# Gated linear attention and a two-level mixture of experts: the first expert in parts of 128 and 88 rows, the second in a fixed place, narrow products on halves of the array's columns

## The chip, the cores and the metric

The kernel runs on one core of a Trainium2 chip. The metric is the device time of one execution in microseconds. Three executions of the kernel before took 394.83, 397.62 and 399.1 us; the median is 397.62. The profile is of one further execution, which took 390.5 us.

The engines are TensorE (PE; its weight loads are listed apart as PEld), VectorE (DVE), ScalarE (ACT), GpSimd (POOL) and SyncE (SP). In this kernel SP issues the plain transfers, all in one order, and POOL issues the indirect ones (scatters), among its own arithmetic.

## What is computed

```python
def _attn_ref(q, k, v, alpha):                  # (4, 8, 768, 48) each
    for t in range(S):
        state = alpha[:, :, t, :, None] * state + np.einsum('bhd,bhe->bhde', k[:, :, t], v[:, :, t])
        y[:, :, t] = np.einsum('bhd,bhde->bhe', q[:, :, t], state)

def _moe_ref(x, w_group, w_expert, w1, w2):     # x (3072, 384), G = Eg = 4, F = 1024
    g_idx = np.argmax(x @ w_group, axis=1)
    # g_w: weight of the chosen group by softmax
    for g in range(G):
        # e_idx: argmax of xg @ w_expert[g], e_w its softmax weight
        for e in range(Eg):
            h = np.maximum(xg[mask_e] @ w1[g, e], 0.0)
            ye = h @ w2[g, e]
            out[tok_idx] = (g_w * e_w)[:, None] * ye
```

The result of the attention, (B, H, S, D) turned to 3072 rows of 384, is the x of the mixture. Each row goes to one of 16 experts. Everything is in float32.

## The kernel before, in words

**First stage, the attention, in 24 steps.** The sequence is cut into chunks of 128 rows, 6 for each of 4 batches; step n treats chunk n. On TensorE a step has these pieces, by the names that the plan gives them: OUT (`outputs`, L506: masked scores times v, in the same banks as FB), G (`gains`, L463: the chunk's addition to the state), SC of the next step (`scores`, L428), TR (`turned_keys`, L446: transposed keys), CNT where a group of chunks is to be counted (L601, L605), ROWS (`to_rows`, L527: the chunk's output turned to rows, and the logits of the gates, in one product), FB of the next step (`from_before`, L494: queries times the state). TR is left out where the next chunk but one begins a batch, G and FB where the next one does. L506, L463 and L494 write some partitions from 0 and some from 64, so they already use parts of the array's columns. One matmul of float32 in the program shows as two in the profile.

Around it: q, k and alpha come in units u = 0 to 10 of one to three chunks (transfers L*u*). DVE makes two scans of alpha for each part of a unit (R, F: L378, L388). ACT scales the queries (QS, L405), and the products KP and QP (`decayed`, L414) are made on POOL, or on DVE where the list `BY_DVE` says so. Each step's scores are masked in two halves M0 and M1: the list `MASKS` says how many of them DVE does straight from PSUM (L433); the others are copied by ACT (MC, L856) and masked on POOL (L437).

**The way to the experts.** For groups of chunks DVE picks each row's expert (PA, PB), weighs it (WT) and, after CNT, gives it a place among the expert's slots (PL). X*t* (`scatter`, L625) on POOL then writes the 128 rows of chunk t to `slots_d` in DRAM. The slots are first filled with blank rows (`fill`, four transfers FILL, L320), and every X waits for all of them.

**The plan.** All pieces of the first stage are `Work` items with an engine, a planned duration, needs and a due time. `in_turns` plays them through with these durations and so fixes the order on every engine before the program is built; TensorE's and SP's orders are given by the text. On the chip each engine then runs its list strictly in that order. Constants such as `FIRST`, `STEP`, `X0`, `XSTEP` and `LOGITS` only shift due times or order; `QUEUE` is the order of SP's transfers.

**Second stage, the experts.** `jobs` is a list of (expert, rows). For each, SP reads its rows (`fetch_rows`), DVE transposes them (`columns`, L1031), TensorE makes `hidden_part` (L237: 8 pieces of F by 3 of the model's width) and `result_part` (L248: 3 by 8), ACT takes both out of PSUM, DVE turns the result back and weighs it, and POOL scatters it (L1023). The matmuls move as many columns as the job has rows. Job 0 and job 1 are expert 0: 96 rows that were in place after 12 chunks (`EARLY`, `EARLY_T`), and 128 more. Job 0's hidden products (E0 to E3) and two thirds of its result (RP) belong to the plan and come at the end of the first stage; its rows are read by ER and transposed by ET. The other 15 experts are ordered by their number of rows (`by_number`) and get ceilings of 216, 213, 210 and so on to 168 (`cap`). A loop at the end treats rows above a ceiling. Weights are in two buffers, filled two jobs ahead (`load_weights`); the first is loaded as LW within the plan, job 2's after `by_number`.

```python
    CAP = 224
    FIXED, EARLY, EARLY_T, BLK = 1, 96, (B // 2) * NC, 112
    jobs = [dict(e=0, n=EARLY, rows=early_rows), dict(e=0, c0=EARLY, n=CAP - EARLY)]
    jobs += [dict(r=r, c0=0, n=cap(r)) for r in range(NS)]
```

On these inputs the experts have 213, 184, 202, 191, 211, 196, 184, 200, 180, 158, 195, 181, 168, 194, 205 and 210 rows. Of expert 0's, 96 lie in the first 12 chunks and 131 in the first 16.

Of the kernel before, what the change touches and what calls it, by code (L numbers as in the profile page):

```python
# [96 lines left out]
def gla_then_hierarchical_moe(  # L97
# [53 lines left out]
    FIXED, EARLY, EARLY_T, BLK = 1, 96, (B // 2) * NC, 112  # L151
# [58 lines left out]
    blank = cp.tile([P, 2 * XW], F32, name="blank")  # L210
# [22 lines left out]
    def hidden_part(z, w1, xt, hT, f0, n, halves=(0, 1)):  # L233
        for k in halves:
            f = f0 + k
            for dc in range(DC):
                nc.tensor.matmul(z[:, k * n:(k + 1) * n], lhsT=w1[:, dc, f * P:(f + 1) * P],  # L237
                                 rhs=xt[:, dc, 0:n], start=(dc == 0), stop=(dc == DC - 1))
# [4 lines left out]
    def result_part(z, w2, hT, yT, d0, n):  # L243
        k = min(2, DC - d0)
        for i in range(k):
            dc = d0 + i
            for f in range(FC):
                nc.tensor.matmul(z[:, i * n:(i + 1) * n], lhsT=w2[:, f, dc * P:(dc + 1) * P],  # L248
                                 rhs=hT[:, f, 0:n], start=(f == 0), stop=(f == FC - 1))
# [19 lines left out]
    with ExitStack() as gla:  # L269
# [22 lines left out]
        nc.scalar.copy(out=blank, in_=zeros[:, 0:1].to_broadcast([P, 2 * XW]))  # L292
# [225 lines left out]
        def to_rows(n, yt):  # L518
# [6 lines left out]
            for p in range(HP):  # L525
                at = p * W - p % 2 * NL
                nc.tensor.matmul(z[:, at:at + W], lhsT=yt[:, p, :], rhs=wr[:, p, :],  # L527
                                 start=(p == 0), stop=(p % 2 == 1), skip_group_check=True)
# [8 lines left out]
        def choose(b, c0, c1):  # L537
# [71 lines left out]
            def place():  # L609
# [3 lines left out]
                if cs.stop == EARLY_T:  # L613
                    nc.vector.tensor_scalar(out=new[:, 0:FIXED], in0=new[:, 0:FIXED],
# [38 lines left out]
        def fill(e, n):  # L653
# [3 lines left out]
                in_=blank[0:CAP // 2, None, :].to_broadcast([CAP // 2, n, 2 * XW]))  # L657
# [3 lines left out]
        def constants():  # L661
# [5 lines left out]
            nc.gpsimd.memset(blank.rearrange("p (k w) -> p k w", w=QW)[:, :, QW - 1:QW],  # L667
                             float(4 * N))
# [35 lines left out]
        FIRST, STEP = 11.19, 4.52  # L704
# [4 lines left out]
        BY_DVE = [('QP', 1, 3), ('KP', 3, 3), ('QP', 4, 2), ('QP', 0, 0), ('QP', 3, 3), ('KP', 0, 0), ('QP', 2, 1), ('QP', 1, 2), ('KP', 0, 2), ('QP', 2, 2), ('QP', 3, 2)]  # L709
# [78 lines left out]
        QUEUE = [('L', 1), ('V', 0, 0, 1), ('L', 2), ('L', 3), ('W',), ('V', 0, 1, 3), ('L', 4), ('V', 0, 3, 6), ('L', 5), ('L', 6), ('V', 1, 0, 6), ('L', 7), ('L', 8), ('V', 2, 0, 6), ('B', 0), ('B', 1), ('B', 2), ('B', 3), ('L', 9), ('V', 3, 0, 6), ('L', 10)]  # L788
# [11 lines left out]
        groups = [(0, 6, 8), (6, 12, 14), (12, 15, 16), (15, 18, 20), (18, 21, 22), (21, 23, 23), (23, 24, 24)]  # L800
# [97 lines left out]
        for n in range(LAST):  # L898
# [30 lines left out]
            on_array(f"ROWS{n}", 0.99, 1.09, keep(f"ROWS{n}", to_rows, n, held(f"YT{n}")),  # L929
# [26 lines left out]
        add("AR", ACT, 0.4, 0.55, lambda: hold["RP"](), ["RP"])  # L956
# [140 lines left out]
    def by_number():  # L1097
# [208 lines left out]
```

## Time and profile before

| | |
|---|---|
| median of three executions | 397.62 us (394.83 to 399.1) |
| the profiled execution | 390.5 us, span of its instructions 388.8 |
| first stage, to the first of the early products | 0 to 116.2 us |
| early products, and job 1 to its end | 116.2 to 141.5 |
| 15 jobs | 141.5 to 378.5 |
| behind TensorE | 378.5 to 388.8 |
| TensorE busy | 374.7 us, 3366 matmuls |
| POOL busy | 195.3 us |
| L1023, scatters of results on POOL | 99, mean 974 ns |
| L625, scatters of rows on POOL | 24, mean 1002 ns |
| L527, ROWS | 192 matmuls, busy 26.1 us |

The time is that of the whole execution, the span runs from the first to the last instruction of the profile. Matmuls overlap, so a mean of one (325 ns on L237) is no pitch: pitches come from the chain of waits, where each piece has the time by which it moved the end, or from a group's length in the timeline.

### The profile page before, as it was taken

What the parts mean: (1) busy time and instruction counts of PE and PEld (TensorE: products, weight loads), DVE (VectorE), ACT (ScalarE), POOL (GpSimd) and SP (SyncE); (2) the same over time, 40 slices, a digit from 0 to 9 for tenths busy, and PEclk for the clock granted to TensorE, in tenths of its full rate; (3) what the DMA queues carried; (4) which work ended last, traced back from release to release, by engine and by line L of the source; (5) the groups of instructions that cost most, each with busy time, mean ns of one, the idle gap of its engine ahead of it and who ended that gap; (6) DMA issues with size and microseconds to landing.
All of it is one profiled execution on the core that took longest, in us unless ns stands there. A gap on an engine that the chain in (4) does not pass through costs nothing.

```text
span 388.8 us, 8864 instructions
## 1 busy us (share of the span) xinstructions
PE 374.7 (96%) x3366; PEld 356.6 (92%) x3366; DVE 162.4 (42%) x420; ACT 139.3 (36%) x379; POOL 195.3 (50%) x240
## 2 busy tenths in 40 slices
PE   8999999999999899999999999999999999999990
PEld 3888998898989899999999999999999999999990
DVE  7999998899868220207322020220201202202200
ACT  5989899596762211111121121211212112112110
POOL 5988886888746321244261633526336235144341
PEclk9999999999999999999999999999999999999996
DMA  8999999994313799986585866768668777665000
GB/s 284 380 410 412 413 358 352 410 417 172 100 64 128 154 328 346 333 244 219 175 255 218 276 220 207 224 227 282 227 201 257 269 245 240 249 250 182 16 22 27
DMA packets 32411, 95.22 MB, mean 245 GB/s; under 512 B 18175, under 2 KB 18454, under 8 KB 27888
## 3 DMA queue, kind: packets, MB, share of 16 engines
q1 hardware_dynamic: 27552, 85.10, 63.5%
q0 software_dynamic: 4816, 9.55, 7.3%
q8 instruction: 27, 0.44, 0.5%
q14 instruction: 16, 0.13, 0.1%
HBM read 79.47 MB, written 15.56 MB: 244 GB/s over the span
## 4 chain that ended last, share of the span: by engine, by line
PE 69%; DMA 18%; issue 5%; POOL 4%; SPq 1%; DVE 1%; POOLq 0%; ACT 0%; DVEq 0%; ACTq 0%
PE bank L237 29%; PE bank L248 29%; DMA slots_d<-blank 7%; DMA qka<-in_qka_dram 5%; DMA w<-in_qka_dram 3%; PE zo L506 3%; PE zs L428 3%; PE bank L527 2%; DMA out_dram<-yq,dst_q 2%; POOL out_dram L1023 1%; DMA v<-in_v_dram 1%; PE zo L494 1%; SPq L320 1%; POOL slots_d L625 1%; PE bank L446 1%
## 5 line engine op out<-in xcount | busy, mean ns | idle before, releaser
L1023 POOL DMA_INDIRECT out_dram<-yq,dst_q x99 | 96.4, 974 | 153.2 <-DVE yq L1019 121.3
L237 PE MATMUL bank<-xt_e,w 128*128 128x128 f32 (+15 forms) x768 | 126.5, 325 | 1.4 <-DVE dst_q L1045 0.8
L248 PE MATMUL bank<-hT,w 128*128 128x128 f32 (+15 forms) x768 | 126.3, 324 | 0.0
L237 PEld LDWEIGHTS bank<-xt_e,w 128*128 128x128 f32 x768 | 124.1, 190 | 1.7 <-PE bank L248 0.9
L248 PEld LDWEIGHTS bank<-hT,w 128*128 128x128 f32 x768 | 124.1, 190 | 0.0
L1040 DVE CAST dst_q<-xq 128x7 int32<-128x7 f32 (+2 forms) x16 | 2.7, 168 | 168.8 <-DMA out_dram<-yq,dst_q 168.8
L239 ACT ACTIVATE hT<-bank 128x256 f32<-128x256 f32 (+15 forms) x64 | 31.3, 489 | 96.3 <-PE bank L237 96.3
L250 ACT COPY yT<-bank 128x256 f32<-128x256 f32 (+31 forms) x32 | 12.7, 398 | 109.0 <-PE bank L248 109.0
L625 POOL DMA_INDIRECT slots_d<-xr,place x24 | 24.1, 1002 | 10.6 <-issue 3.3
L506 PE MATMUL zo<-sm,v 128*48 128x128 f32 (+1 forms) x384 | 27.2, 280 | 1.0 <-POOL sm L437 1.0
L428 PE MATMUL zs<-qp,kp 48*128 48x128 f32 x384 | 28.2, 285 | 0.0
L527 PE MATMUL bank<-wr,yt 112*128 112x116 f32 x192 | 26.1, 279 | 0.5 <-ACT sm L856 0.5
L506 PEld LDWEIGHTS zo<-sm,v 128*48 128x48 f32 (+1 forms) x384 | 20.3, 129 | 6.5 <-POOL sm L437 2.4
L428 PEld LDWEIGHTS zs<-qp,kp 48*128 48x128 f32 x384 | 23.4, 187 | 2.6 <-DVE qp L414 0.8
L527 PEld LDWEIGHTS bank<-wr,yt 112*128 112x128 f32 x192 | 23.3, 191 | 0.9 <-ACT sm L856 0.7
L405 ACT ACTIVATE w<-w,whole 112x128 f32<-112x128 f32 x60 | 19.8, 402 | 2.0 <-DMA w<-in_qka_dram 2.0
L378 DVE TENSOR_TENSOR_SCAN rev<-w,starts 112x387 f32<-112x387 f32 (+1 forms) x22 | 18.5, 869 | 3.4 <-DMA w<-in_qka_dram 3.4
L414 POOL TENSOR_TENSOR kp<-w,rev 112x384 f32<-112x384 f32 (+1 forms) x21 | 18.3, 886 | 2.2 <-DVE rev L378 2.0
L414 POOL TENSOR_TENSOR qp<-w,cq 112x384 f32<-112x384 f32 (+1 forms) x20 | 17.1, 862 | 4.4 <-ACT w L405 3.9
L433 DVE TENSOR_TENSOR sm<-zs,causal 128x512 f32<-128x512 f32 x28 | 18.3, 679 | 2.4 <-PE zs L428 2.2
L388 DVE TENSOR_TENSOR_SCAN cq<-w,starts 112x387 f32<-112x387 f32 (+1 forms) x22 | 19.1, 871 | 0.0
L1016 DVE STREAM_TRANSPOSE yq<-yT 128x672 f32<-128x672 f32 (+2 forms) x15 | 12.3, 818 | 15.5 <-ACT yT L250 15.4
(135 smaller groups left out, 340.6 us busy)
## 6 DMA issues: line engine op xcount, KB each, us to landing
w<-in_w_dram SPq DMA_DIRECT2D x32, 1536.0 KB, 7.1
w<-in_qka_dram SPq DMA_DIRECT2D x16, 578.0 KB, 10.4
slots_d<-blank SPq DMA_DIRECT2D x4, 1372.0 KB, 19.1
qka<-in_qka_dram SPq DMA_DIRECT2D x8, 578.0 KB, 12.7
v<-in_v_dram SPq DMA_DIRECT2D x3, 1152.0 KB, 15.8
xq<-slots_d SPq DMA_DIRECT2D x32, 85.8 KB, 7.6
qka<-in_qka_dram SPq DMA_DIRECT2D x6, 385.5 KB, 6.3
xq<-slots_d SPq DMA_DIRECT2D x28, 73.5 KB, 6.3
```

Source lines behind the costliest of these rows:

```text
L237: nc.tensor.matmul(z[:, k * n:(k + 1) * n], lhsT=w1[:, dc, f * P:(f + 1) * P], rhs=xt[:, dc, 0:n], start=(dc == 0), stop=(dc == DC - 1))
L239: return lambda: nc.scalar.activation(out=hT[:, f0:f0 + 2, 0:n], in_=z[:, 0:2 * n].rearrange("p (f t) -> p f t", f=2), func=AF.Relu)
L248: nc.tensor.matmul(z[:, i * n:(i + 1) * n], lhsT=w2[:, f, dc * P:(dc + 1) * P], rhs=hT[:, f, 0:n], start=(f == 0), stop=(f == FC - 1))
L378: nc.vector.tensor_tensor_scan(out=part_of("rev", u, i, A1).rearrange("r c s -> r (c s)")[:, ::-1], data0=a[:, W:0:-1], data1=one_col.to_b ...
L388: nc.vector.tensor_tensor_scan(out=cq, data0=a[:, 0:n * A1], data1=starts[0:R, 0:n * A1], initial=1.0, op0=ALU.mult, op1=ALU.min)
L405: nc.scalar.activation(out=q[:, j, :], in_=q[:, j, :], func=AF.Copy, scale=ready["whole", u][:, i * g + j // k, c:c + 1])
L414: engine.tensor_tensor(out=part_of(kind, u, i, P), in0=of, in1=by[:, :, 1:A1], op=ALU.mult)
L428: nc.tensor.matmul(z[i][:, p, :], lhsT=kp[r, p, c, :], rhs=qp[r, p, c, :], start=True, stop=True)
L506: nc.tensor.matmul(of(z, p)[o], lhsT=vs[b][:, bc, h * D:h * D + o.stop - o.start], rhs=sm[:, i, p, :], start=(p < 2 and bc == 0), stop=Tru ...
L527: nc.tensor.matmul(z[:, at:at + W], lhsT=yt[:, p, :], rhs=wr[:, p, :], start=(p == 0), stop=(p % 2 == 1), skip_group_check=True)
L625: dma = nc.gpsimd.indirect_dma_start(out=slots_by[cs.start + c], out_offset=bass.IndirectOffsetOnAxis(ap=it["to"][:, c:c + 1], axis=0), in ...
L1023: nc.gpsimd.indirect_dma_start(out=out_by.popleft().rearrange("n (j w) -> (n j) w", j=4), out_offset=bass.IndirectOffsetOnAxis(ap=dst[:, b ...
```

## The change

- `hidden_part` and `result_part` make a product of fewer than 128 columns as two, each with 64 columns of the weights and into partitions 0 to 63 or 64 to 127. Of the jobs this concerns job 1.
- ROWS does the same with its 128 columns of `yt`.
- Expert 0 has a ceiling of 216 in place of 224: 128 rows early (from the first 16 chunks) and 88. The early result is made whole in RP.
- Expert 1 is job 2, with a ceiling of 188. Its weights are loaded in the plan (LX), behind ER, and its rows are read without waiting for the order by number. The other 14 experts are ordered as before, with the ceilings 216 to 171.
- The plan's constants are new: `QUEUE` (the four fills between loads, v earlier), `MASKS`, `BY_DVE`, two groups counted one step earlier, `X0` and `XSTEP`, `LOGITS`, and 0.3 for 0.4 in `in_turns`.

```diff
@@ in_turns
-            if not any(now < t < now + w.takes - 0.4 and y.due < w.due and y.due < now + w.takes
+            if not any(now < t < now + w.takes - 0.3 and y.due < w.due and y.due < now + w.takes
@@
-    FIXED, EARLY, EARLY_T, BLK = 1, 96, (B // 2) * NC, 112
+    FIXED, EARLY, EARLY_T, BLK = 2, P, (B // 2) * NC + 4, 112
+    FIXED_CAPS = [CAP - 8, CAP - 36]
+    halves = [slice(0, 64), slice(64, P)]
@@
-    def hidden_part(z, w1, xt, hT, f0, n, halves=(0, 1)):
-        for k in halves:
-            f = f0 + k
+    def sides(n):
+        return [slice(0, P)] if n >= P else halves
+
+    def hidden_part(z, w1, xt, hT, f0, n, of=(0, 1)):
+        for k in of:
+            at = (f0 + k) * P
             for dc in range(DC):
-                nc.tensor.matmul(z[:, k * n:(k + 1) * n], lhsT=w1[:, dc, f * P:(f + 1) * P],
-                                 rhs=xt[:, dc, 0:n], start=(dc == 0), stop=(dc == DC - 1))
+                for x in sides(n):
+                    nc.tensor.matmul(z[x, k * n:(k + 1) * n],
+                                     lhsT=w1[:, dc, at + x.start:at + x.stop],
+                                     rhs=xt[:, dc, 0:n], start=(dc == 0), stop=(dc == DC - 1))
@@ result_part (the same for w2)
-    def result_part(z, w2, hT, yT, d0, n):
-        k = min(2, DC - d0)
+    def result_part(z, w2, hT, yT, d0, n, k=2):
+        k = min(k, DC - d0)
@@ to_rows
-                nc.tensor.matmul(z[:, at:at + W], lhsT=yt[:, p, :], rhs=wr[:, p, :],
-                                 start=(p == 0), stop=(p % 2 == 1), skip_group_check=True)
+                for x in halves:
+                    nc.tensor.matmul(z[x, at:at + W], lhsT=yt[:, p, x], rhs=wr[:, p, :],
+                                     start=(p == 0), stop=(p % 2 == 1), skip_group_check=True)
@@
-        FIRST, STEP = 11.19, 4.52
+        FIRST, STEP = 11.30, 4.47
-        BY_DVE = [('QP', 1, 3), ('KP', 3, 3), ('QP', 4, 2), ('QP', 0, 0), ('QP', 3, 3), ('KP', 0, 0), ('QP', 2, 1), ('QP', 1, 2), ('KP', 0, 2), ('QP', 2, 2), ('QP', 3, 2)]
+        BY_DVE = [('QP', 1, 3), ('QP', 4, 2), ('QP', 3, 3), ('QP', 3, 2), ('KP', 4, 3), ('KP', 3, 3), ('KP', 1, 3), ('KP', 3, 0), ('KP', 2, 2), ('QP', 0, 3), ('KP', 1, 2), ('KP', 2, 3)]
@@
-        QUEUE = [('L', 1), ('V', 0, 0, 1), ('L', 2), ('L', 3), ('W',), ('V', 0, 1, 3), ('L', 4), ('V', 0, 3, 6), ('L', 5), ('L', 6), ('V', 1, 0, 6), ('L', 7), ('L', 8), ('V', 2, 0, 6), ('B', 0), ('B', 1), ('B', 2), ('B', 3), ('L', 9), ('V', 3, 0, 6), ('L', 10)]
+        QUEUE = [('L', 1), ('V', 0, 0, 1), ('V', 0, 1, 3), ('L', 2), ('W',), ('L', 3), ('V', 0, 3, 6), ('L', 4), ('L', 5), ('L', 6), ('V', 1, 0, 6), ('B', 0), ('L', 7), ('B', 1), ('L', 8), ('B', 2), ('V', 2, 0, 6), ('B', 3), ('L', 9), ('V', 3, 0, 6), ('L', 10)]
@@
         queued("ER", 2.0, 5.0, read_early, [f"X{EARLY_T - 1}"])
+        lent = max(u for u in range(NU) if (u + 1) % 3 == 1)
+        queued("LX", 7.5, 9.5, lambda: load_weights(2, 1, in_turn), each("KP", lent) + each("QP", lent))
@@
-        groups = [(0, 6, 8), (6, 12, 14), (12, 15, 16), (15, 18, 20), (18, 21, 22), (21, 23, 23), (23, 24, 24)]
+        groups = [(0, 6, 8), (6, 12, 13), (12, 15, 15), (15, 18, 20), (18, 21, 22), (21, 23, 23), (23, 24, 24)]
@@
-        MASKS = [1, 0, 0, 1, 1, 1, 0, 2, 0, 0, 1, 1, 1, 2, 1, 2, 2, 2, 2, 2, 2, 2, 1, 1]
-        X0, XSTEP = 96.8, 1.90
+        MASKS = [1, 0, 0, 1, 1, 1, 0, 2, 0, 0, 1, 1, 1, 2, 1, 2, 2, 2, 2, 2, 2, 1, 2, 0]
+        X0, XSTEP = 64.7, 3.08
-        LOGITS = 20
+        LOGITS = 0
@@
-            on_array(f"ROWS{n}", 0.99, 1.09, keep(f"ROWS{n}", to_rows, n, held(f"YT{n}")),
+            on_array(f"ROWS{n}", 0.87, 0.97, keep(f"ROWS{n}", to_rows, n, held(f"YT{n}")),
@@
-        on_array("RP", 3.0, 3.2, lambda: hold.update(RP=result_part(
-            bank(), weights[0][1], early_hT, early_xt, 0, EARLY)), ["A0", "A1", "A2", ("A3", 0.6)],
-            readers=["AR"])
+        on_array("RP", 5.2, 5.4, lambda: hold.update(RP=result_part(
+            bank(), weights[0][1], early_hT, early_xt, 0, EARLY, DC)),
+            ["A0", "A1", "A2", ("A3", 0.6)], readers=["AR"])
@@
-    jobs = [dict(e=0, n=EARLY, rows=early_rows), dict(e=0, c0=EARLY, n=CAP - EARLY)]
+    jobs = [dict(e=0, n=EARLY, rows=early_rows), dict(e=0, c0=EARLY, n=FIXED_CAPS[0] - EARLY),
+            dict(e=1, c0=0, n=FIXED_CAPS[1])]
@@
-            if k == 2:
+            if k == 3:
                 order, excess, ceiling = by_number()
@@
-        w1, w2 = weights[0] if j < 2 * FIXED else weights.pop(j)
+        w1, w2 = weights[0] if j < 2 else weights.pop(j)
@@
         if j == 0:
-            result_part(bank(), w2, early_hT, early_xt, 2, EARLY)()
...
-            tc.add_manual_dep(load_weights(2, expert(jobs[2])), fetched, mybir.DependencyInfo(
-                mybir.DependencyClass.NoSync, mybir.DependencyReason.SCHED_ONLY),
-                reason="the rows go ahead of the weights")
```

Built, POOL's list in the middle of the first stage changes like this (before, then after):

```
QP8.1 M1.12 QP8.2 X0 QP8.3 X1 KP9.0 X2 M1.14 KP9.1 X3 KP9.2 KP9.3 X4 QP9.0 X5 QP9.1 QP9.2 X6 QP9.3 X7
M1.12 QP8.1 X0 QP8.2 X1 QP8.3 X2 KP9.0 M1.14 X3 KP9.1 KP9.2 X4 KP9.3 X5 QP9.0 QP9.1 X6 QP9.2 X7 QP9.3
```

and its end like this:

```
X10 QP10.0 QP10.1 X11 QP10.2 QP10.3 X12 X13 X14 X15 M1.22 X16 X17 M1.23 X18 X19 X20 X21 X22 X23
X10 QP10.0 QP10.1 X11 QP10.2 X12 QP10.3 X13 M1.21 X14 X15 X16 X17 M0.23 M1.23 X18 X19 X20 X21 X22 X23
```

More of the change, by code (lines that the diff above doesn't have):

```diff
@@ L209, in gla_then_hierarchical_moe @@
     picked = cp.tile([P, NT, NE], BF16, name="picked")
-    blank = cp.tile([P, 2 * XW], F32, name="blank")
+    blank = cp.tile([P, max(2 * XW, FC * EARLY)], F32, name="blank")
     seen = cp.tile([P, NT + 1, NE], F32, name="seen")
@@ L241, in hidden_part @@
             func=AF.Relu)
-    def result_part(z, w2, hT, yT, d0, n):
-        k = min(2, DC - d0)
+    def result_part(z, w2, hT, yT, d0, n, k=2):
+        k = min(k, DC - d0)
         for i in range(k):
-            dc = d0 + i
+            at = (d0 + i) * P
             for f in range(FC):
-                nc.tensor.matmul(z[:, i * n:(i + 1) * n], lhsT=w2[:, f, dc * P:(dc + 1) * P],
-                                 rhs=hT[:, f, 0:n], start=(f == 0), stop=(f == FC - 1))
+                for x in sides(n):
+                    nc.tensor.matmul(z[x, i * n:(i + 1) * n],
+                                     lhsT=w2[:, f, at + x.start:at + x.stop],
+                                     rhs=hT[:, f, 0:n], start=(f == 0), stop=(f == FC - 1))
         return lambda: nc.scalar.copy(out=yT[:, d0:d0 + k, 0:n],
@@ L291, in gla_then_hierarchical_moe @@
                            in_=zeros[0:R, 0:1].to_broadcast([R, HP * 64]))
-        nc.scalar.copy(out=blank, in_=zeros[:, 0:1].to_broadcast([P, 2 * XW]))
+        nc.scalar.copy(out=blank[:, 0:2 * XW], in_=zeros[:, 0:1].to_broadcast([P, 2 * XW]))
         nc.scalar.copy(out=quarters[:, :, :, QW - 1], in_=quarter_f)
@@ L613, in place @@
                 if cs.stop == EARLY_T:
-                    nc.vector.tensor_scalar(out=new[:, 0:FIXED], in0=new[:, 0:FIXED],
+                    nc.vector.tensor_scalar(out=new[:, 0:1], in0=new[:, 0:1],
                                             scalar1=float(EARLY), scalar2=None, op0=ALU.max)
@@ L656, in fill @@
                     "e (p t) w -> p e (t w)", t=2),
-                in_=blank[0:CAP // 2, None, :].to_broadcast([CAP // 2, n, 2 * XW]))
+                in_=blank[0:CAP // 2, None, 0:2 * XW].to_broadcast([CAP // 2, n, 2 * XW]))
         later = {}
@@ L666, in constants @@
                            allow_small_or_imprecise_dtypes=True)
-            nc.gpsimd.memset(blank.rearrange("p (k w) -> p k w", w=QW)[:, :, QW - 1:QW],
-                             float(4 * N))
+            nc.gpsimd.memset(blank[:, 0:2 * XW].rearrange("p (k w) -> p k w", w=QW)
+                             [:, :, QW - 1:QW], float(4 * N))
         PE, DVE, ACT, POOL, SP = ENG.PE, ENG.DVE, ENG.Activation, ENG.Pool, ENG.SP
@@ L952, in gla_then_hierarchical_moe @@
         early(3)
-        on_array("RP", 3.0, 3.2, lambda: hold.update(RP=result_part(
-            bank(), weights[0][1], early_hT, early_xt, 0, EARLY)), ["A0", "A1", "A2", ("A3", 0.6)],
-            readers=["AR"])
-        add("AR", ACT, 0.4, 0.55, lambda: hold["RP"](), ["RP"])
+        on_array("RP", 5.2, 5.4, lambda: hold.update(RP=result_part(
+            bank(), weights[0][1], early_hT, early_xt, 0, EARLY, DC)),
+            ["A0", "A1", "A2", ("A3", 0.6)], readers=["AR"])
+        add("AR", ACT, 0.5, 0.65, lambda: hold["RP"](), ["RP"])
         all_ = {name: Work(e, takes, serves, emit, (), due)
@@ L1118, in by_number @@
         excess, ceiling = (rp.tile([P, NE], F32, name=k) for k in ("excess", "ceiling"))
-        nc.vector.memset(ceiling[:, 0:FIXED], float(CAP))
+        for e, n in enumerate(FIXED_CAPS):
+            nc.vector.memset(ceiling[:, e:e + 1], float(n))
         nc.vector.tensor_scalar(out=ceiling[:, FIXED:NE], in0=rank, scalar1=float(cap(1) - cap(0)),
@@ L1178, in gla_then_hierarchical_moe @@
         for k in range(1 if j == 0 else j + AHEAD, j + AHEAD + 1):
-            if k == 2:
+            if k == 3:
                 order, excess, ceiling = by_number()
             if k < len(jobs):
-                dma = fetch_rows(jobs[k])
-                if k == 2:
-                    fetched = dma.ins.name
+                fetch_rows(jobs[k])
         width = job["n"]
-        w1, w2 = weights[0] if j < 2 * FIXED else weights.pop(j)
+        w1, w2 = weights[0] if j < 2 else weights.pop(j)
         dst = destined(job)
         if j == 0:
-            result_part(bank(), w2, early_hT, early_xt, 2, EARLY)()
             last = (job, early_xt, dst)
```

## The prediction

> **What bounds the kernel now.** I read the busy times by stretch, then the chain of waits, then the timeline at the places where the chain leaves TensorE. By stretch (columns: busy us and count of PE, PEld, DVE, ACT, POOL; clock; DMA share; GB/s):
>
> ```profile
> 0.00:76.00 76.00, 73.30 (x1061) 60.57 (x1063) 68.31 (x152) 63.25 (x186) 60.59 (x100) 1.00 0.99 377
> 76.00:116.20 40.20, 40.20 (x664) 35.96 (x659) 34.89 (x112) 28.50 (x87) 29.97 (x33) 1.00 0.52 201
> 116.20:141.50 25.30, 23.53 (x208) 22.88 (x206) 11.12 (x54) 5.13 (x15) 9.30 (x11) 1.00 0.62 186
> 141.50:378.50 237.00, 237.00 (x1442) 236.81 (x1442) 47.50 (x105) 41.58 (x90) 93.52 (x96) 1.00 0.69 226
> ```
>
> After 76 us TensorE never rests but for 1.8 us between 116 and 141. Before 76 us it is nearly full, yet the DMA engines are too (0.99), and the chain goes through them:
>
> ```profile
> 42.86 25.34 DMA slots_d<-blank
> ...
> 69.17 0.99 POOL slots_d L625
> 70.15 0.22 issue
> 70.37 0.80 POOL qp L414
> ...
> 71.47 1.01 POOL slots_d L625
> ...
> 74.62 0.65 POOL sm L437
> 75.28 0.04 issue
> 75.32 0.65 PE zo L506 x7
> ```
>
> The last fill of the slots lands at 68.20; X0, the first scatter, waits for it on POOL, and the mask M1.14 stands behind X0 to X2. The timeline puts 0.70 us of TensorE idle on that mask:
>
> ```profile
> 75.32 0.65 PE L506 MATMUL zo<-sm,v 128*64 128x128 f32 x8 [0.70 <-POOL sm L437]
> 127.09 2.02 PE L248 MATMUL bank<-blank,w 128*128 128x96 f32 x16 [0.41 <-ACT early_xt L250]
> 129.73 5.62 PE L237 MATMUL bank<-xt_e,w 128*128 128x128 f32 x48 [0.61 <-DVE dst_q L1040]
> 141.47 3.71 PE L237 MATMUL bank<-xt_e,w 128*128 128x216 f32 x19 [0.76 <-DVE dst_q L1045]
> ```
>
> So steps 0 to 14 are paced by transfers and POOL, the rest by TensorE. The chain also prices TensorE's pieces:
>
> ```profile
> 82.40 0.53 PE bank L446 x4
> 82.93 0.90 PE bank L527 x8
> ...
> 92.30 1.02 PE zo L506 x16
> 93.32 0.45 PE bank L463 x15
> ...
> 159.22 8.64 PE bank L237 x48
> 167.86 8.64 PE bank L248 x48
> 176.50 8.52 PE bank L237 x48
> ```
>
> Three columns fewer (213 to 210) save 0.12 us in 48 matmuls: 0.833 ns a column, 180 ns at 213. The 96-wide job does not follow: 24 of its matmuls take 2.90 us in the timeline, and 48 of 128 columns 5.62, some 112 to 114 ns each. [...]
>
> [...] L506 and L463 already use column halves [...]: 16 matmuls of 128 columns in 1.02 us are 64 ns each, 16 of 48 columns 28 ns. [...] X11 starts at 98.11 and the read behind it is issued at 100.93, 2.8 later.
>
> **Part by part**, against the profiled execution (span 388.8, run 390.5).
>
> *POOL's order, steps 0 to 14.* Built, POOL has between M1.12 and M1.14: QP8.1, X0, QP8.2, X1, QP8.3, X2, KP9.0; before, one product fewer followed X0. SP's queue now spreads the fills among the loads, but the same transfers stand ahead of the last fill (the third batch of v and everything before it), and the DMA engines were full, so I let it land at 68.2 again. X0 then starts at 69.2, and M1.14 comes one product later: 0.92 (the L414 row in the timeline) plus 0.12 between two entries, **+1.04**. What changes earlier on any engine, the cheaper start included, disappears in this wait: TensorE stood here 0.70. Late loads of u=7, u=8 and v wait two or three fills longer (some 4.8 us each by the fills' 19 us together), against scans that follow their landing by 6 to 8 us. Bounds: −2 (the fill lands early enough for POOL never to wait, and early stalls of TensorE count too) to +2.
>
> *Steps 14 to 23.* CNT1 moves from step 14 to 13, ahead of the wait: 0.04 + 0.17 from the chain, **−0.2**. ROWS: 16 matmuls on halves, interpolated from L506 [...]: 1.02 − 8 × 12 × 0.833 ns = 0.94. Before it took 0.90 behind TR (L446[...]) and 0.98 behind CNT. Half of these ten steps are of each kind: **0**. Bounds: −0.1 or +0.1 a step, [...] so ±1.0. POOL now mixes the scatters earlier: 12 entries instead of 11 before QP9.3, one more before QP10.3. By the old pitches (product 0.92, scatter 1.1) QP9.3 ends near 90 and QP10.3 near 103.5; SC18 and SC21 want them at 91.5 and 104.7. Hidden by that.
>
> *The early part.* It reads 16 tiles instead of 12. X15 stands behind M1.21, which needs SC21 (ends 104 before), a copy of 0.58 and 0.64 on POOL: with +1.0, X14 at 106.6 and X15 at 107.9. X11 started at 98.11 and ET, at the end of that chain, at 106.21: 8.1 us. ET could start at 116.0. On DVE it stands behind LG22 and PA5 (115.85 before, 116.7 now), so its rows have 0.7 us to spare; but ET itself (0.58, as the 128x384 transpose) now ends 0.25 after E0.0 could start: **+0.25**, bounds 0 and +2. E0.0 starts at 116.2 + 1.1 = 117.3. The products of 128 rows cost what 96 cost (112 ns floor). One bank takes all of RP, so the stall of 0.41 goes, but not the time: job 1 needs the last scatter's rows. ROWS23, LG23, gates, X23, xq: 13.54 us from E0.0 to job 1, less 0.11 for a smaller transpose (0.47 for 0.58): job 1 at 130.7. TensorE would be ready at 129.8; the stall is now some 0.9 there.
>
> *Job 1*, 88 rows on halves. Before: 141.47 − 0.76 − 129.73 = 10.98 us. Now 96 pairs; L506's 1.09 us for 16 in the timeline, less its last 0.28 (mean of one), is 7 pairs at 116 ns [...], near 109 [...] (128 x 0.833 and some 2); 40 columns fewer give 76 to 83: 7.5 us, **−3.5**. Bounds −3.7 and −2.2 (92 ns, between L463 and L506 in a straight line).
>
> *Job 2* is the second expert; its weights (LX) go into the second buffers behind ER, near 112, and have 18 us. Before, SP issued w1 at 132.41, and with a median of 7.1 it landed no sooner than 139.5; whether that or dst_q held job 2, neither is left: **−0.76** (0 to −0.76). LX runs beside the scatters X16 to X20 when the DMA engines were idle; X23 comes after it.
>
> *Columns from job 2 on:* 15 jobs with 2913 before; 188 and 14 jobs with 2739, 2927, now. 14 × 96 × 0.833 ns = **+1.1**. Job 3's weights may load once job 1 is through, 15 us ahead. The last job has 171 columns, not 168; the 10 us behind TensorE stay. No expert is over its new ceiling on these inputs (213 of 216, 184 of 188), so the loop for left-over rows stays empty.
>
> Sum: +1.04 − 0.2 + 0.25 − 0.11 − 3.5 − 0.76 + 1.1 = **−2.2**, 386.6 of span, 388.3 the run. The three times have a median 1.8% above the profiled run; in that ratio 397.62 becomes **395.4**.
>
> **Rivals.** *Faster:* the spread fills land sooner or their skew is absorbed, POOL doesn't wait, and halves save 0.1 a step: −1.0 − 2.0 − 1.0 more, 391.3 to 392.5. For it: X0 waits 3.25 us in the timeline. Against: the bytes ahead of the last fill are the same. *Slower:* one mechanism, the early rows' chain X15, ER, ET. It has 0.7 us to spare; every further microsecond stands on E0.0, on ROWS23 and so on job 1. From X15 at 110.8 on (2.9 late) the gain is gone; if POOL's denser stretch brings X15 at 113.5, the end is 2.7 later, 400.4. For it: 14 scatters now precede M1.21 on POOL, 16 before M1.22 had been reached with 1.8 us gaps. Against: POOL was 75% busy after 76 us. *The halves do not overlap:* job 1 takes 192 × 58 ns = 11.1 and ROWS gains nothing: 399.5. L463's 28 ns speak against it.
>
> **Numbers.** Sum as worked 0.50, faster 0.27, slower chain 0.18, no overlap 0.05. The likeliest's own range is 393 to 398 (ROWS ±1, wait ±1). About 1%, 4 us, is what a measurement of this kernel tells from no change. Faster by over 1% (under 393.6): most of the second case and an eighth of the first, 0.28; slower by over 1% (over 401.6): half of the last two with the spread of the runs, 0.16; the rest 0.56. The range reaches into both rivals: 390 to 401.
>
> **What would show it.** M1.14 ending near 76.3 and TensorE's longest wait of the stage there; ROWS near 0.94 in the chain; ET near 116.8 and E0.0 right behind; a stall near 0.9 before job 1; its 96 pairs in 7.5; no stall before job 2. It is wrong if the fill lands away from 68, if ET waits for its rows, or if ROWS is off by more than 0.1.

## The result, and the profile after

Five runs of the changed kernel: **407.18 us** median (405.30 to 408.66), five of the kernel before beside them 397.62 (394.52 to 399.44): ratio **1.0265, 95% interval 1.0218 to 1.0312**, slower. Forecast were 395.4 and a range of 390 to 401.

The profiled execution took 407.62, its span is 405.9. Busy times by stretch (columns as before: PE, PEld, DVE, ACT, POOL with counts; clock; DMA share; GB/s):

```profile
0.00:76.00 76.00, 72.67 (x1187) 58.87 (x1187) 68.99 (x155) 63.80 (x187) 61.88 (x102) 1.00 0.99 383
76.00:116.20 40.20, 39.13 (x642) 33.38 (x639) 31.35 (x93) 25.86 (x80) 27.94 (x30) 0.93 0.57 217
116.20:141.50 25.30, 20.66 (x215) 19.34 (x214) 12.52 (x63) 6.36 (x17) 8.33 (x10) 0.83 0.45 154
141.50:378.50 237.00, 234.51 (x1532) 233.72 (x1529) 47.85 (x108) 41.12 (x90) 90.43 (x93) 0.99 0.68 224
```

The first row has no loss. The second and third have a clock of 0.93 and 0.83 where there was 1.00. The timeline shows the place where it begins, in step 22 (start, us, engine, what; in brackets the idle time before and what ended it):

```profile
107.14 0.30 PEld L438 LDWEIGHTS zs<-qp,kp 48*128 48x128 f32 x4
107.71 0.32 PEld L438 LDWEIGHTS zs<-qp,kp 48*128 48x128 f32 x4 [0.28 <-issue]
108.25 0.97 POOL L636 DMA_INDIRECT slots_d<-xr,place  x1 [0.30 <-issue]
108.44 0.41 PEld L438 LDWEIGHTS zs<-qp,kp 48*128 48x128 f32 x5 [0.40 <-issue]
...
109.25 0.59 ACT L524 COPY yt<-zo 112x512 f32<-112x512 f32 x1 [2.49 <-remote]
109.52 0.98 POOL L636 DMA_INDIRECT slots_d<-xr,place  x1 [0.30 <-issue]
...
111.32 1.45 PEld L538 LDWEIGHTS bank<-wr,yt 112*64 112x64 f32 x14 [0.99 <-issue]
111.50 0.35 DVE L482 TENSOR_TENSOR gained<-state,bank 112x192 f32<-112x192 f32 x1 [3.96 <-PE bank L456]
```

TensorE does four or five weight loads, rests 0.3 to 1.0 us, does some more, and waits for nothing that the profile knows ("issue"). ACT and DVE start 2.5 and 4 us after the products that they wait for ("remote": the profile finds no releaser among this core's instructions). At 110.96 the clock falls to half, for 6.83 us, so the fall comes after the pauses and not ahead of them. I call this a *halt*. There are two more: CNT6 waits 4.08 us because LG23, the step on DVE ahead of it, starts 3.42 us late, and job 1 looks like this:

```profile
140.86 3.10 PE L244 MATMUL bank<-xt_e,w 128*64 128x88 f32 x74 [0.57 <-ACT early_xt L260]
144.34 0.36 PE L244 MATMUL bank<-xt_e,w 128*64 128x88 f32 x2 [0.38 <-issue]
145.08 0.39 PE L244 MATMUL bank<-xt_e,w 128*64 128x88 f32 x4 [0.38 <-issue]
...
147.98 0.45 PE L244 MATMUL bank<-xt_e,w 128*64 128x88 f32 x6 [1.04 <-issue]
...
148.28 5.50 PE L257 MATMUL bank<-hT,w 128*64 128x88 f32 x95
```

The first 74 matmuls take 84 ns a pair: the halves do overlap. Then come the pauses, then half clock. Job 1 takes 12.86 us; 7.5 were forecast.

### The profile page after: what moved, and what is told of

Its sections match the earlier page's. It is cut to its first block, busy times and chain, and to the rows that moved or that the text cites. A ratio compares the mean times of both kernels' runs of the same rounds, so it can differ in the third digit from the quotient of the medians.

```text
span 405.9 us, 9433 instructions
## 1 busy us (share of the span) xinstructions
PE 381.1 (94%) x3654; PEld 358.9 (88%) x3654; DVE 162.7 (40%) x420; ACT 140.3 (35%) x379; POOL 197.0 (49%) x242
## 4 chain that ended last, share of the span: by engine, by line
PE 82%; DMA 4%; issue 4%; POOL 3%; DVE 2%; SPq 1%; another core or an unknown queue 1%; ACT 1%; POOLq 0%; ACTq 0%
PE bank L257 30%; PE bank L244 30%; PE zs L438 5%; PE bank L538 5%; PE zo L516 5%; DMA w<-in_qka_dram 4%; PE zo L504 2%; PE bank L456 2%; PE bank L473 2%; POOL qp L424 1%; SPq L330 1%; POOL out_dram L1036 1%; POOL out_dram L1021 1%; ACT w L415 0%
## 5 line engine op out<-in xcount | busy, mean ns | idle before, releaser
L244 PE MATMUL bank<-xt_e,w 128*64 128x88 f32 (+15 forms) x816 | 126.6, 318 | 3.1 <-issue 2.5
L244 PEld LDWEIGHTS bank<-xt_e,w 128*128 128x128 f32 (+1 forms) x816 | 123.5, 184 | 4.0 <-issue 3.2
L257 PE MATMUL bank<-hT,w 128*64 128x88 f32 (+15 forms) x816 | 126.9, 324 | 0.0
L257 PEld LDWEIGHTS bank<-hT,w 128*128 128x128 f32 (+1 forms) x816 | 124.7, 189 | 0.0
L247 ACT ACTIVATE hT<-bank 128x176 f32<-128x176 f32 (+15 forms) x64 | 31.1, 485 | 98.0 <-PE bank L244 68.4
L260 ACT COPY yT<-bank 128x176 f32<-128x176 f32 (+31 forms) x32 | 12.6, 395 | 109.6 <-PE bank L257 109.6
L438 PE MATMUL zs<-qp,kp 48*128 48x128 f32 x384 | 30.3, 292 | 2.2 <-POOL qp L424 1.8
L538 PE MATMUL bank<-wr,yt 112*64 112x116 f32 x384 | 25.7, 274 | 0.6 <-issue 0.6
L538 PEld LDWEIGHTS bank<-wr,yt 112*64 112x64 f32 x384 | 19.9, 140 | 3.6 <-issue 1.0
L1029 DVE STREAM_TRANSPOSE yq<-yT 128x672 f32<-128x672 f32 (+2 forms) x15 | 12.2, 812 | 22.4 <-ACT yT L260 22.4
L447 POOL TENSOR_SCALAR_AFFINE_SELECT sm<-sm 128x512 f32<-128x512 f32 x21 | 13.0, 634 | 12.4 <-DVE bank L628 8.7
```

The costliest lines, as they stand in the source:

```text
L244: nc.tensor.matmul(z[x, k * n:(k + 1) * n], lhsT=w1[:, dc, at + x.start:at + x.stop], rhs=xt[:, dc, 0:n], start=(dc == 0), stop=(dc == DC ...
L247: return lambda: nc.scalar.activation(out=hT[:, f0:f0 + 2, 0:n], in_=z[:, 0:2 * n].rearrange("p (f t) -> p f t", f=2), func=AF.Relu)
L257: nc.tensor.matmul(z[x, i * n:(i + 1) * n], lhsT=w2[:, f, at + x.start:at + x.stop], rhs=hT[:, f, 0:n], start=(f == 0), stop=(f == FC - 1))
L438: nc.tensor.matmul(z[i][:, p, :], lhsT=kp[r, p, c, :], rhs=qp[r, p, c, :], start=True, stop=True)
L538: nc.tensor.matmul(z[x, at:at + W], lhsT=yt[:, p, x], rhs=wr[:, p, :], start=(p == 0), stop=(p % 2 == 1), skip_group_check=True)
```

## The experiments

Kernels that ran together share a chip and their own runs of the kernel before, whose median was 399.42, 389.73, 389.32, 397.16 and 389.65 us in the five sets. The last three ran on one and the same chip with 389.32, 397.16 and 389.65, so the chip alone is not the difference. "Changed" in this part is the changed kernel with one edit. Theory 1: the halves put more instructions on TensorE than it gets or can retire. Theory 2: the new order or the early fetch of job 2's weights (LX). Theory 3: a limit of clock or power of the chip. Theories 4 to 6 came later, and stand where they were formed.

### Set 1: is it the halves? (before: 399.42)

`b_same` is the kernel before, unchanged.

> The kernel before, unchanged, as a run of its own: its profiled execution was 4 to 9 us faster than all its timed ones, and only that one has a clock and a trace. If TensorE's stall of the changed kernel is new, every execution here has a clock of 0.99 or more and a span within 3 us of 388.8. If the kernel before has it too, in some executions, then spans near 393 to 398 come with clocks of 0.98 or less.

Measured: 399.22 us, twelve executions with spans of 396.1 to 400.4 and clocks of 0.977 to 0.984. The kernel before halts too. Its timeline, step 21:

```profile
102.99 0.97 POOL L625 DMA_INDIRECT slots_d<-xr,place  x1 [0.30 <-issue]
103.76 0.41 PE L428 MATMUL zs<-qp,kp 48*128 48x128 f32 x3 [0.21 <-issue]
104.27 0.97 POOL L625 DMA_INDIRECT slots_d<-xr,place  x1 [0.31 <-issue]
...
105.28 0.38 PE L428 MATMUL zs<-qp,kp 48*128 48x128 f32 x2 [0.35 <-issue]
106.01 0.82 PE L428 MATMUL zs<-qp,kp 48*128 48x128 f32 x9 [0.35 <-issue]
106.15 0.58 ACT L514 COPY yt<-zo 112x512 f32<-112x512 f32 x1 [3.73 <-remote]
```

The same pauses, the same late copy. So theory 2 falls as the cause of halting as such: this kernel has neither the new order nor LX. The execution that the prediction was worked out from (390.5, clock 0.992) has none of these pauses; the timed runs beside it (394.5 to 399.4) lie between it and the upper end of these. Three kernels undo the halves:

```
a_rows_full (L538)   -  for x in halves:
                     +  for x in [slice(0, P)]:
a_job1_full (sides)  -  return [slice(0, P)] if n >= P else halves
                     +  return [slice(0, P)]
a_both_full          both
```

> The changed kernel with the rows' product (L538) on the whole array again, 8 matmuls a step and not 16; order, plan and transfers unchanged. Theory 1 (the halves put more instructions on TensorE than it can be supplied with or can retire, so that it halts from time to time; the clock's fall follows): steps 21 and 22 run at 4.5 us again, no half clock near 111, the span loses 6 to 12 us, 394 to 400. Theory 2 (the new order, the early fetch of job 2's weights or the crowded scatters hold it up): the slow stretch from 107 to 118 stays, span 404 to 407. Theory 3 (a fall of the clock of its own, that no instruction causes): the same as theory 2.

> The changed kernel with job 1 (88 rows) on the whole array, 96 matmuls and not 192; the rows' product stays on halves. Theory 1: the stretch from 107 to 130 stays as it is, job 1 takes 48 x 112 ns twice, 10.8 us, without halting, instead of 12.9: span about 404. Theory 2: the pause inside job 1 stays, whose cause is the order or a transfer: job 1 takes 14 us or more, span 407. Theory 3: as theory 2.

> The changed kernel with no halves in either place: what is left is the split 128 and 88, the second expert in a fixed place with its weights fetched early, and the new plan. Theory 1: none of the three slow stretches, clock 0.99, span 388 to 392 (the 386.6 that the prediction had, and 3.3 for job 1 at full width). Theory 2: the slow stretches near 107 and 123 stay, 400 or more.

Measured: 404.91 (ratio 1.0142, 1.0089 to 1.0194), 407.31 (1.0191, 1.0143 to 1.0238) and 405.01 (1.0125, 1.0064 to 1.0185). All three halt at the first place, and at CNT6 they wait 1.6, 4.3 and 1.6 us. With no halves at all:

```profile
108.99 0.97 POOL L636 DMA_INDIRECT slots_d<-xr,place  x1 [0.30 <-issue]
109.26 0.51 PE L438 MATMUL zs<-qp,kp 48*128 48x128 f32 x4 [0.25 <-issue]
110.00 0.38 PE L438 MATMUL zs<-qp,kp 48*128 48x128 f32 x2 [0.23 <-issue]
110.26 0.98 POOL L636 DMA_INDIRECT slots_d<-xr,place  x1 [0.30 <-issue]
```

Theory 1 falls as the cause of the first two halts. In job 1 it holds in part: with the halves (`a_rows_full`) it has six pauses, 2.5 us together, half clock from 144.09 on, and lasts 12.96 us; at full width (`a_job1_full`) it has one wait of 0.69 for a late signal of ACT, full clock, and lasts 11.72. Both times go to the start of job 2. Where TensorE halts, the halves lose a microsecond there instead of winning three.

### Set 2: is it the scatters? (before: 389.73)

In every halt POOL sends scatters in a row, 1.28 us apart, and TensorE's pauses end 0.66 to 0.99 us after the last one has ended (first halt, in the end nine traces), so I formed **theory 4**: such a row holds TensorE and the signals up. Fills of a scratch tile space the scatters. `a_mute` leaves X14 to X17 out and has six fills in the place of each, so the rows of these four tiles never reach their experts; its time is that of a kernel with less to do.

```
+    def rest(k=5):
+        for _ in range(k):
+            nc.gpsimd.memset(spare, 0.0)        # 128 x 160
...
                 sent.append(dma.ins.name)
+                if 14 <= cs.start + c < 17:      # a_gap; a_gap_all and b_gap_all: more of them
+                    rest()
```

> The changed kernel with some 0.8 us of fills of a small scratch tile on POOL behind each of the scatters X14, X15 and X16, so that the four scatters X14 to X17, which follow each other at 1.28 us, stand 2.1 apart as the earlier ones do. Theory 4 (a row of scatters at 1.28 us holds up TensorE and the signals between engines while it lasts, and what halts falls to half clock): no halt of TensorE at steps 21 and 22, no half clock near 111; OUT22 near 110.3 and OUT23 near 114.8 and not 114.1 and 120.1; the halts near 123 and in job 1 stay, as their rows of scatters do; span 396 to 401 for 405.9. Theory 1 (instructions too dense, by themselves): the halt near 107 stays, span 404 to 408. Theory 3 (a clock or power limit some 105 us after the start): it stays too.

> The changed kernel with the scatters X14 to X17 left out (the rows of these four tiles are not placed) and POOL kept busy for as long with fills of a scratch tile. Theory 4: the halt at steps 21 and 22 is gone as in the spaced version, so it is the scatters and not POOL being busy. If it stays, POOL's pace or TensorE itself is the cause, and theory 4 falls.

> The changed kernel with such fills behind X14 to X16, X18 to X21 and three of the four scatters of job 0's results, so that no two scatters follow each other at 1.28 us before job 2. Theory 4: no halt at steps 21 and 22, no wait of 4 us of CNT6, job 1 in about 8 us; clock 0.99; X22 lands some 3 us later than its place in the row, which costs 0 to 3 before job 1: span 387 to 392, as the prediction's sum had it. Theories 1 and 3: at most 2 us are won.

> The kernel before with the same fills behind X12, X13, X16 and X18 to X21. Theory 4: its own halt near 103 and the wait of 3 us for CNT6 go as well, clock 0.99, span 387 to 391 for 397 to 400. Theories 1 and 3: span 396 to 400 as before.

Measured: 396.49 (1.0183, 1.0153 to 1.0213), 388.90 (0.9996, 0.9972 to 1.0020), 400.34 (1.0281, 1.0255 to 1.0307) and 396.45 (1.0179, 1.0153 to 1.0204). No halt in any of them, but the kernel before, at 389.73 with clocks of 0.990 to 0.993, shows that nothing halted in this set anyway: it tells nothing of theory 4, against what the expectations had. It does give a price: `b_gap_all` sends X23 at 127.68 instead of 122.46, and job 1 starts at 134.59 instead of 129.73. The 5.2 us of X23 are 4.9 of job 1.

### Set 3: the changed kernel where nothing halts (before: 389.32)

`a_gap2` has two fills and not five behind X14 to X16; `a_mute2` is `a_mute` with three fills and not six in the place of each scatter; `a_early` sends X11 three times more, into scratch tensors.

> The changed kernel, unchanged, beside the variants on one chip. The kernel before took 399 us on one chip and 390 on another, where it has no halt. Theory 4 (rows of scatters hold TensorE up, but only on some chips): where the kernel before takes 390, this one takes what its instructions ask for, the sum's 386 to 391 of span, clock 0.99, 387 to 393 us; where it takes 399, this one takes 405 to 408. Theory 1 (the density of instructions on halves): it halts on every chip, 403 to 408.

> The changed kernel with 0.6 us of fills on POOL behind X14, X15 and X16 (pitch 2.05 us for 1.28). Where the kernel before takes 399: theory 4 says no halt at steps 21 and 22, 4 to 8 us less than the changed kernel; theory 3 (a limit of the chip some 105 us after the start) says that it halts all the same. Where before takes 390: 0 to 2 us more than the changed kernel, for POOL's later mask.

> The changed kernel with X14 to X17 left out (the rows of four tiles are not placed) and 0.9 us of fills on POOL in the place of each. Where before takes 399: no halt at steps 21 and 22 by theory 4, a halt by theory 3. Where before takes 390: within 1 us of the changed kernel, 388 to 390.

> The changed kernel with the scatter X11 done four times in a row, three of them into scratch tensors that nothing reads: a row of four at 98 to 103 us, where the changed kernel had single scatters with products of POOL between. POOL's last products come 3.8 us later, which holds TensorE up for some 3 us near 103 on every chip. Where before takes 399: theory 4 says that TensorE halts (pauses that nothing explains, signals 2 to 4 us late) between 99 and 104, until 1 us after the fourth; theory 3 says no halt before 105.

Measured: 394.52 (1.0143, 1.0104 to 1.0183), 395.87 (1.0189, 1.0141 to 1.0236), 389.43 (1.0001, 0.9985 to 1.0017), 396.53 (1.0191, 1.0138 to 1.0243). No halt, not in the extra row of `a_early` either, which has 2.2 us of waits for POOL's late products. So **the change costs 1.4% with no halt at all**, which no theory so far had. The span of `after_same` is 391.1, and its stretches after 76 us are:

```profile
76.00:116.20 40.20, 40.20 (x721) 34.83 (x717) 34.46 (x109) 29.28 (x89) 29.77 (x34) 1.00 0.57 216
116.20:141.50 25.30, 23.14 (x320) 22.68 (x319) 10.11 (x48) 4.75 (x14) 9.98 (x11) 0.93 0.79 239
141.50:378.50 237.00, 236.30 (x1432) 235.80 (x1430) 48.52 (x109) 41.93 (x91) 92.37 (x95) 1.00 0.65 215
```

Steps 14 to 21 are unbroken, and one clock fall is left, between 116 and 141. I set the starts in the traces of before (388.8) and of this one side by side:

| from, to | before | changed | difference | forecast |
|---|---|---|---|---|
| start to E0.0, the first early product | 116.19 | 115.35 | -0.84 | +1.09 |
| E0.0 to job 1 | 13.54 | 14.48 | +0.94 | -0.11 |
| job 1, with the wait behind it | 11.74 | 9.08 | -2.66 | -4.26 |
| job 2 to the end of the last product | 236.71 | 237.86 | +1.15 | +1.1 |
| behind it, to the end | 10.62 | 14.33 | +3.71 | 0 |
| sum | 388.8 | 391.1 | +2.3 | -2.2 |

Two places are open. **Ahead of job 1**, the chain of waits of `after_same`:

```profile
127.70 0.49 ACT early_xt L260
128.19 1.64 issue
129.83 5.51 PE bank L244 x96
135.34 3.64 PE bank L257 x96
```

The second half of job 1 takes 3.64 us, the first 5.51, at half clock from 129.91 to 133.32. The clock fell right behind the 2.17 us in which TensorE stood still ahead of the job. What it waits for is seen in the transfers:

```profile
111.25 0.84 SPq L330 DMA_DIRECT2D w<-in_w_dram  x2
114.87 0.99 POOL L636 DMA_INDIRECT slots_d<-xr,place  x1 [0.16 <-issue]
...
121.55 0.97 POOL L636 DMA_INDIRECT slots_d<-xr,place  x1 [0.57 <-ACT blank L247]
...
125.90 5.00 SPq L1165 DMA_DIRECT2D xq<-slots_d  x9
...
129.83 1.48 PE L244 MATMUL bank<-xt_e,w 128*64 128x88 f32 x17 [2.17 <-issue]
```

Job 1's rows (L1165) are asked for 4.35 us after X23's start; in the kernel before it was 2.80. Counted from the packets of POOL's queue, X18, sent at 114.87, moves nothing until 119, and the six scatters are through at 125. In front of them stand the 3 MB of LX, sent at 111.25: **theory 5**, that they hold up the scatters sent after them, X18 here by some 4 us. `a_mute` shows the other case by a side effect: without X14 to X17 the early rows, and LX behind them, go out 4.2 us earlier.

```profile
107.02 1.69 SPq L336 DMA_DIRECT2D w<-in_w_dram  x2
...
115.36 0.99 POOL L645 DMA_INDIRECT slots_d<-xr,place  x1 [0.16 <-issue]
...
122.03 0.97 POOL L645 DMA_INDIRECT slots_d<-xr,place  x1 [0.57 <-ACT blank L253]
...
124.89 6.03 SPq L1174 DMA_DIRECT2D xq<-slots_d  x11
...
128.79 2.42 PE L250 MATMUL bank<-xt_e,w 128*64 128x88 f32 x58 [0.64 <-ACT early_xt L266]
```

X18's packets move from 116 on, the rows are asked for 2.86 us after X23's start, TensorE waits 0.64, the clock stays whole, and the hidden and the result products of job 1 take 3.66 and 3.77 us: the 7.5 of the forecast. The traces of `a_gap` and `a_gap2` show the other end. `a_gap2`:

```profile
121.71 0.97 POOL L642 DMA_INDIRECT slots_d<-xr,place  x1 [0.60 <-ACT blank L253]
...
128.01 7.89 SPq L1173 DMA_DIRECT2D xq<-slots_d  x14
...
131.92 5.13 PE L250 MATMUL bank<-xt_e,w 128*64 128x88 f32 x96 [4.09 <-issue]
```

The rows are asked for 6.30 us after X23's start here, 5.52 in `a_gap` and 4.35 in `after_same`; in these three X23 starts 9.9, 10.0 and 10.3 us after LX is sent. In every other trace of a changed kernel with LX in this place X23 starts 12.5 us or more after it, and the rows follow in 2.7 to 3.0.

**Behind the last product** of the experts the last scatter is the difference. It has 171 - 112 = 59 rows where it had 168 - 112 = 56: **theory 6**. The last two scatters of `after_same` have 400 packets where those of `before` have 112, so the theory is that 59 rows are cut into many tiny packets, and that these cost the time.

### Set 4: both places put right (before: 397.16)

```
a_tail     cap(r):  - (6 if r >= NS - 2 else 0)   ->  (9 if r >= NS - 2 else 0)    174, 171 -> 171, 168
b_59       the same line of before: 6 -> 3                                         171, 168 -> 174, 171
a_lx_late  - queued("LX", ...);  w1 of job 2 behind job 1's rows, its w2 behind job 2's
a_best     a_tail and a_lx_late
```

> The changed kernel with the last two of the ranked jobs at 171 and 168 columns (they had 174 and 171), so that the last scatter has 56 rows, as in the kernel before, and not 59. Theory 6 (59 rows are cut into many tiny packets): the last scatter's packets fall from 400 to 112, the span behind the last product of L257 from 14.3 to 10.6 us, and 0.5 us less for six columns: 4.2 us less than the changed kernel. Rival (the end is longer for another reason, as the longer program): 0.5 us less.

> The changed kernel with job 2's weights fetched behind the rows of job 1 (first half) and of job 2 (second half), not behind the early rows. Theory 5 (the 3 MB stand in front of the scatters X18 to X23, whose data so land late): X18 to X23 land within 2 us of their issue, the rows of job 1 are asked for near 124.5 instead of 125.9, TensorE waits 0.8 us ahead of job 1 instead of 2.2, no half clock there, job 1 takes 7.5 us instead of 9.1, and job 2 waits 0 to 1.5 for its weights: 1.5 to 3 us less than the changed kernel on a chip where the kernel before takes 389. Rival (the wait before job 1 has another cause, as the choice of the last tile): no change there, and 0 to 2 us more for the weights.

> Both of these edits. If both theories hold the gains add up, 5.5 to 7 us: span 384 to 386 where the changed kernel has 391 and the kernel before 388; 387 us for 394.5 and 389.3. If only theory 6 holds, 390.

> The kernel before with its last two jobs at 174 and 171 columns (they had 171 and 168), so that its last scatter has 59 rows and not 56: one part of the change alone. Theory 6: 400 packets instead of 112, 3.7 us at the end and 0.5 for six columns, 4.2 us slower than the kernel before. Rival: 0.5 slower.

Measured: 400.17 (1.0087, 1.0059 to 1.0115), 403.39 (1.0173, 1.0084 to 1.0262), 399.02 (1.0108, 1.0043 to 1.0173) and 400.27 (1.0129, 1.0050 to 1.0208). TensorE halts in all four traces, so the totals are to be read with care; the end is not touched by that. POOL's last scatter in `before`, `after_same`, `b_59` and `a_tail`, from the timelines:

```profile
381.31 0.94 POOL L1008 DMA_INDIRECT out_dram<-yo,dst_m  x1 [0.30 <-issue]
```

```profile
379.90 1.65 POOL L1021 DMA_INDIRECT out_dram<-yo,dst_m  x1 [0.30 <-issue]
```

```profile
386.60 1.65 POOL L1008 DMA_INDIRECT out_dram<-yo,dst_m  x1 [0.30 <-issue]
```

```profile
390.32 0.94 POOL L1021 DMA_INDIRECT out_dram<-yo,dst_m  x1 [0.30 <-issue]
```

and the packets of POOL's queue (packets, MB, share of the engines) for the last two scatters, in the same order:

```profile
q0 software_dynamic: 112, 0.24, 8.8%
```

```profile
q0 software_dynamic: 400, 0.25, 7.6%
```

```profile
q0 software_dynamic: 400, 0.25, 7.8%
```

```profile
q0 software_dynamic: 112, 0.24, 8.5%
```

With 59 rows the bytes are the same within 2%, the packets 400 for 112: 288 of them have 12 bytes, where there were 4. From the end of the last product to the end of the span there are 10.6, 14.3, 14.8 and 10.2 us. **Theory 6 is shown from both sides**: 59 rows cost some 4 us in the kernel before, and 56 take them away from the changed one. `b_59` is 3.1 us slower than before by the medians; 4.2 were expected. The last scatter's packets are through 6.1 us after its start in `after_same` and 2.3 in `before`, and with 59 rows those of 4608 bytes come one after the other, 0.18 us apart, where with 56 several start within 0.04 us. The profile doesn't name engines, so it isn't shown how many of them work on either.

Theory 5 was not tested here: X23 comes so late (128.74 in `a_tail` and 129.02 in `a_lx_late`, by the halt at CNT6) that even in `a_tail` LX has long landed, and the rows follow by 2.74 and 2.80 us. `a_best` missed its expectation: nothing stands in front of X23 in its trace, and still the last packets of X23 come at 133 for a start at 129.83, the rows are asked for 4.86 us after it, and TensorE waits 3.17 us ahead of job 1. That is one trace against theory 5 as the only cause, and why is open.

### Set 5: spaced scatters once more (before: 389.65)

`a_tail_gap` is `a_tail` with two fills behind seven of the scatters X14 to X21 and three of job 0's results, `b_gap_short` the kernel before with two fills behind seven.

> The changed kernel with its last two jobs at 171 and 168 columns (56 rows in the last scatter) and with 0.6 us of fills on POOL behind X14 to X16, X18 to X21 and the first three scatters of job 0's results, so that the scatters of a row stand 2.05 us apart and not 1.28. Where TensorE halts (the kernel before at 397 to 399 beside it): theory 4 says no halts at 107, at CNT6 or in job 1, span 386 to 391, where the same kernel without the fills had 397.4; theory 3 (a limit of the chip that depends on time) says that the halts stay, 397 to 401. Where it doesn't halt (the kernel before at 389 to 390): 388 to 391, up to 3 us for the later X22 and X23.

> The kernel before with the same fills behind X12, X13, X16 and X18 to X21. Where TensorE halts: theory 4 says 389 to 393 us instead of 397 to 399, no half clock between 100 and 135; theory 3 says 397 to 402. Where it doesn't: 390 to 393 us instead of 389 to 390.

Measured: 391.06 (1.0040, 1.0018 to 1.0062) and 393.93 (1.0090, 1.0057 to 1.0123). Nothing halted beside them, so theory 4 was again not put to the test. X23 goes out at 125.48 and 125.35, 3 to 4 us late, TensorE waits 3.75 and 2.91 ahead of job 1 and falls to half clock. `a_tail_gap` is the nearest that the changed kernel came to the kernel before, 1.4 us by the medians where `after_same` was 5.2 behind; the 3.8 between them are about what the end with 56 rows takes away. No version that places all rows beat the kernel before.

## Why the prediction was wrong

The forecast of 388.3 for the profiled run became 395.4 by a ratio of 1.8%. Where nothing halts, the profiled run took 392.8: 4.5 more than the sum. Where it halts, 407.6: 14.8 more again, for which the ratio had 7.1. 4.5 + 14.8 - 7.1 is the error, 12.2 (11.8 against the median). Three steps cost this: the end behind TensorE, the fetch LX beside the scatters, and the ratio, which is the largest part. Luck hides some of it: the time to E0.0 was 1.9 us better than the sum had it, as the rival "faster" had named; without that the sum would have been off by 6.4.

- **"The last job has 171 columns, not 168; the 10 us behind TensorE stay."** This step failed and is the largest error of the sum, 3.7 us. The 10.6 became 14.3: the 171 columns are 112 rows and 59, and with 59 rows the last two scatters go as 400 packets and not as 112. Shown by `b_59` and `a_tail`. I had counted the columns as matmul time and not as rows of a scatter.
- **"LX runs beside the scatters X16 to X20 when the DMA engines were idle; X23 comes after it."** Failed. The engines were idle, but X18 to X23 then stood behind LX, and the read of job 1's rows behind X23. The stall ahead of job 1 is 2.17 us, not 0.9, and the clock falls behind it. This rests on traces (the rows 4.35 to 6.30 us after X23 in three, 2.86 and 2.87 in `a_mute` and `a_mute2`) and not on an edit made for it, which came where it could tell nothing; `a_best` does not fit.
- **Job 1 in 7.5 us**: right in mechanism and size at full clock, 7.43 in `a_mute`, or 76 and 79 ns a pair. In `after_same` half clock adds 1.65; in the profiled run of 407.6 pauses and half clock add 5.4. The forecast had no term for the clock.
- **"+1.04" for M1.14 behind a fill at 68.2**: wrong. X0 starts at 67.09 and not 69.2, with no wait for a fill, and the mask is done at 74.25:

```profile
67.09 1.17 POOL L636 DMA_INDIRECT slots_d<-xr,place  x1 [0.18 <-DVE starts L579]
...
73.61 0.64 POOL L447 TENSOR_SCALAR_AFFINE_SELECT sm<-sm 128x512 f32<-128x512 f32 x1
```

  The same bytes ahead of the last fill did not mean the same landing: its last packet ends at 65.53 in this trace and at 63.90 in `after_same`, where it was 67.84 before. TensorE's old wait of 0.70 is gone: E0.0 starts 0.84 earlier, not 1.09 later.
- **ROWS at 0.94**: right, 0.94 in 17 of its 19 pieces in the chain; the others are the 1.79 of the first halt and the last, 1.20. The bounds of 0.1 a step were an estimate. **ET**: its rows are in time, as forecast, but the +0.25 was not there: it is done 0.4 us before E0.0 and sets nothing. **Job 2** starts without a wait: right. **Columns +1.1**: right, 1.15.
- **The ratio of 1.8%** was taken as a spread of runs. This step failed and is the largest part of the error, 7.7 us. By set 1 it is the kernel before halting, which its profiled execution didn't; the timed runs have no trace, so for them this is inferred from their times, beside medians of 389.3 in a calm set and 399.4 in a halting one. The changed kernel loses more by that (394.5 and 407.2), above all in job 1 (12.86 us for 9.08, where the kernel before has 10.75 for 11.74), whose halves run under the scatters of job 0's results.

Of the rivals, "slower" named the chain X15, ER, ET: X15 starts at 106.23, far from the 110.8 where it would decide. "No overlap" is out by the 76 to 84 ns a pair. "Faster" was right that POOL wouldn't wait.

**What stays open.** Why TensorE halts. The coincidence with rows of scatters holds in nine traces that halt, and the same rows run without a halt in the calm sets (`after_same`: four in a row from 104.94, no pause). Spaced or left-out scatters never ran where TensorE halted. The nine traces themselves speak against a row as the whole cause: from 156 to 372 us POOL sends twelve rows of six or seven scatters in each of them, at the same 1.28 us, and TensorE has no pause over 0.15 us there but one in each of three traces. The matmuls there move 168 to 216 columns, some 140 to 180 ns each; those of the first halt take 68 ns, and those of job 1 on halves some 40. Short matmuls and a row of scatters may be needed together; no run tests that. Late instructions from memory don't show: in `a_both_full` and `a_rows_full` no packet of the queues that the profile calls "instruction" moves between 106.5 and 113.7, around all pauses of the first halt. Nor do slower transfers: packets of 12,288 bytes from 150 us on take 544 to 552 ns on average where TensorE halts, 543 to 553 elsewhere. Theory 3 is not excluded, and neither is a hold-up of instructions behind these transfers.

## What to carry to other kernels

Count the rows of every indirect transfer after a change of block sizes: here 59 rows in place of 56 cost some 4 us in the last transfer, which nothing hides. Idle transfer engines are no reason to give them 3 MB (in `after_same` the next scatter's first packet moved some 4 us after it was sent): ask which small transfer comes next and who waits for that. And when timed runs are longer than the profiled one, look at the clock and the trace of a second execution before you turn the difference into a ratio.

## What was not expected of the hardware

- Pauses of TensorE that no wait explains, in bursts of four or five matmuls every 0.72 us, with signals to ACT and DVE 2 to 4 us late, in both kernels, in some sets and not in others, on the same chip.
- A pause of 2.17 us was followed by half clock for 3.41 us (`after_same`, ahead of job 1). All half-clock pieces between the start and the last product are one or two times 3.41 us; in the profiled run they last 6.83, 6.83 and 3.41. In `b_59` one came behind a pause of 1.54 us ahead of CNT6, while one of 1.82 us ahead of job 1 in `a_rows_full` had none behind it. So the length of a pause alone doesn't decide.
- A scatter of 59 rows: 400 packets and 1.65 us of POOL instead of 112 and 0.94, with 2% more bytes (two scatters together).
